# A decode block on Trainium2: the first 1,024 columns of w_o loaded in 12 DMAs of 5 to 18 rows instead of as part of one DMA of 128 rows

## The chip, the cores and the metric

The kernel runs on one core of one Trainium2 chip. The metric is device time in microseconds (us) of one execution, 376.72 us before the change, the median of two runs (376.61 and 376.82). Inside the core, work is issued by separate engines: TensorE (PE in the profile, its weight loads PEld), VectorE (DVE), ScalarE (ACT), GpSimd (POOL), and SyncE (SP), whose queue here does nothing but start DMAs. The data is moved by 16 DMA engines; the profile gives their mean busy share.

## The reference

Two tokens (B = 2) of width D = 448 go through one decode step. All data is fp32.

```python
xn = layernorm(x)                                   # no scale, no shift
q  = (xn @ wq)        -> 16 heads of 256             # wq: 448 x 4096
scores = q . k_cache^T / 16; p = softmax(scores)    # 8 kv heads, 4096 positions, 2 query heads share one kv head
o  = p . v_cache                                    # k_cache, v_cache: 2 x 8 x 4096 x 256 each
s  = o @ wo                                         # wo: 4096 x 448
g  = silu(((xn @ w_gate) * (xn @ w_up)) @ w_down)   # 448 x 1792, 448 x 1792, 1792 x 448
out = x + s * g
```

Almost all of the data is the two caches: 2 x 8 x 4096 x 256 x 4 B = 67 MB each, read once, 134 of the 158.5 MB that the kernel reads.

## The kernel before

There are 16 units of attention, one for each kv head and token, numbered i = 0 to 15. For a unit the keys are a [128, 8192] tile and the values another. The host packs the values of unit i beside the keys of unit i + 1, so that one DMA of [128, 16384] fp32 (8.4 MB, a row of 65,536 bytes for each of 128 partitions) brings both; there are 14 of these, named `vk` in the profile. They go into the pool `ring`, which has two buffers. The first keys (`first`), and the last keys and values (`last0`, `last1`, in 2 and 7 pieces), come apart. The weights (`wq0`, `w_gate` with `w_up`, `w_down`, `wq1` with a small piece `wqx`, `wo`) go one after the other through the pool `slot`, which has one buffer.

All these loads are started on one queue, SP's, by `issue()` (L73 and L77 of the profile), which takes them from a list `todo` in the order in which `plan()` (below it) has put them there. `wo` stands in the list behind the load of v8 and k9 and ahead of the load of v9 and k10. It is a [128, 10752] tile: 24 blocks of 448 columns, one block for each 128 rows of the reference's wo.

The schedule is written by hand (`manual_schedule`): each engine runs its instructions in the order of the code. Semaphores and waits are not in the code; the tile framework adds them, for data that must have arrived, for buffers that must be free, and for its own semaphores. A DMA that must wait holds up what stands behind it on SP.

In pass i of the main loop PE multiplies the probabilities of unit i with its values (`values`, L274), then the queries with the keys of unit i + 1 (`scores`, L243), then `issue()` puts the next load or two on SP's queue; the load into a ring buffer waits for the scores that free it. DVE and ACT compute the softmax of unit i + 1 beside this. In pass 7 the loads `wo` and v9 with k10 are put on the queue, in pass 8 the load of v10 with k11. `wo` is first used at the end of pass 8, by `project` (L301), 16 blocks, and again behind the loop. After the loop come the last two units, the last projections and the output store (L373), which SP starts.

Of the kernel before, what the change touches and what calls it, by code (L numbers as in the profile page):

```python
# [13 lines left out]
B, D = 2, 448  # L14
# [12 lines left out]
LATE = 24  # L27
# [2 lines left out]
SIDE = 16  # L30
EXTRA = 8
EPS = 1e-5

# [4 lines left out]
def gated_decode_block(ctx: ExitStack, tc: tile.TileContext, x, first, vk, last0, last1, wq0, wq1, wqx, wo, wgu, wd, out):  # L40
    nc = tc.nc
# [20 lines left out]
    def issue(n=1):  # L62
        for names, src, cuts in todo[:n]:
            weight = names[0].startswith("w")
            if weight:
                t = slot.tile([128, PART], F32, name="slot", align_bytes=512)
            else:
                t = ring.tile([128, 2 * ROW], F32, name="ring", align_bytes=512)
            width = ROW if not weight else PART // len(names)
            for i, name in enumerate(names):  # L70
                loaded[name] = t[:, i * width:(i + 1) * width]
            for lo, hi in zip(cuts, cuts[1:]):
                nc.sync.dma_start(t[:, lo:hi], src[:, lo:hi])  # L73
            if names == ["wq1"]:
                at = src.shape[1]
                loaded["wqx"] = t[:, at:at + EXTRA * 512]
                nc.sync.dma_start(loaded["wqx"][:SIDE], wqx[:, :4])  # L77
        del todo[:n]

    def plan(names, src, cuts=None):  # L80
        todo.append((names.split(), src, cuts or [0, src.shape[1]]))

    plan("wq0", wq0)
    plan("k0", first)
    weights = {0: ("wg wu", wgu), 2: ("wd", wd), 4: ("wq1", wq1), 8: ("wo", wo)}
    for i in range(LAST):
        plan(f"v{i} k{i + 1}", vk[i])
        if i in weights:
# [1 line left out]
    plan(f"k{LAST + 1} v{LAST}", last0, [0, ROW, 2 * ROW])  # L90
    plan(f"v{LAST + 1} wo2", last1, [0, 4096, 7168, *(ROW + i * D for i in (0, 3, 5, 7, 8))])
    issue(3)


# [20 lines left out]
    nc.vector.scalar_tensor_tensor(sq, xc, 1.0, xc, op0=OP.mult, op1=OP.mult, accum_out=st[:, 2:3])  # L115
    nc.vector.tensor_scalar(st[:, 3:4], st[:, 2:3], 1.0 / D, EPS, op0=OP.mult, op1=OP.add)
    rstd = const.tile([B, 1], F32)
# [16 lines left out]
    for j in range(NK):  # L134
        at = 384 + j * SIDE
# [65 lines left out]
    def lift(ps):  # L201
        t = work.tile([128, D], F32, name="h")
        nc.scalar.copy(t, ps[:, :D])
        return t
# [108 lines left out]
    oT2 = const.tile([128, 1, 2, REP, W], F32)  # L313
    ss = scores(0)
    issue(2)
    p = over(softmax(*ss))
    for i in range(LAST):
        g, b = divmod(i, B)
        o = bank("o", 1)
        values(i, p[0], o)  # L320
        ss = scores(i + 1)

        issue(1 + (i + 1 in weights))
        nc.scalar.activation(ob[:, b * 4 + g if g < 4 else b * 3 + g - 4], o, AF.Copy, scale=p[1])  # L324
        if i == LAST - 1:
            cb = combine(ob, 6)
        p = softmax(*ss)
        if i < LAST - 1:
            p = over(p)
        if i == 7:  # L330
            cb = combine(ob, 8)
            for n in range(B):
                turn(oT0, cb[:, n * 256:(n + 1) * 256], 0, n, 4)
            ob = work.tile([128, 8, 512], F32, name="ob", bufs=1)
        if i in weights:
            if i == 0:
                ffn_in()
            if i == 2:
                ffn_out()
            if i == 4:  # L340
                query(1)
            if i == 8:
                project(oT0, 0, 0, EARLY)
# [6 lines left out]
    t = lift(wide)  # L350
# [72 lines left out]
```

## Time and profile before

The profiled execution took 376.59 us, of which 374.8 us is the span from its first instruction to its last.

| | |
|---|---|
| time, median of 2 runs | 376.72 us (376.61 to 376.82) |
| profiled execution | 376.59 us |
| its span | 374.8 us |
| read from memory | 158.54 MB, mean 424 GB/s over the span |
| PE busy | 207.3 us, 55% of the span |
| PEld, DVE, ACT busy | 61.8, 63.2, 36.2 us |
| POOL busy | 1.2 us |
| the chain that ended last | DMA 79%, PE 19%, SP's queue 1% |

The page has a strip of 40 slices with the busy share of each engine and of the DMA engines, a list of groups of instructions with the time that the engine waited ahead of them and for whom, and the chain of work that ended last. Other views list the instructions of one engine by time, who waited for whom, and, for chosen stretches of time, the busy time of each engine, the mean share of the 16 DMA engines and the rate. A DMA packet is counted in the stretch in which it starts, so that a short stretch can show a share over 1.

### The profile page before, as it was taken

How to read it: one execution, taken by the hardware profiler on the slowest of the kernel's cores; microseconds unless marked ns; L12 is line 12 of the kernel's file. 1: busy time of each engine (PE TensorE's matmuls, PEld its weight loads, DVE VectorE, ACT ScalarE, POOL GpSimd, SP SyncE). 2: the span in 40 equal slices, each digit the busy share in tenths (PEclk: the TensorE clock that was granted, in tenths of full speed). 3: DMA queues.
4: the chain of work that ended last, by engine and by line, in shares of the span. 5: the costliest groups of instructions: out<-in, count | busy, mean ns of one | idle time of the engine just before them, and what ended most of it. 6: DMA issues, size and time to landing. Idle time of an engine off the chain costs nothing.

```text
span 374.8 us, 3254 instructions
## 1 busy us (share of the span) xinstructions
PE 207.3 (55%) x1464; PEld 61.8 (16%) x1464; DVE 63.2 (17%) x113; ACT 36.2 (10%) x56; POOL 1.2 (0%) x7
## 2 busy tenths in 40 slices
PE   1550648081762928678374666642718191909775
PEld 0110112020210202112121211200202020202222
DVE  4012030103030030300303030300211203020530
ACT  1001020001012020100101010200010101010120
POOL 1000000000000000000000000000000000000000
PEclk9987596778686667886758695865968776877999
DMA  8999999998999999999999999999999999999994
GB/s 340 440 465 399 430 453 448 448 442 377 428 442 441 441 403 465 414 448 435 427 448 441 442 415 407 440 448 448 441 428 421 441 441 413 435 416 437 411 418 168
DMA packets 4245, 158.74 MB, mean 424 GB/s; under 512 B 502, under 2 KB 632, under 8 KB 1144
## 3 DMA queue, kind: packets, MB, share of 16 engines
q1 hardware_dynamic: 4228, 158.54, 98.1%
q8 instruction: 11, 0.18, 0.2%
q14 instruction: 2, 0.02, 0.0%
q10 hardware_dynamic: 4, 0.00, 0.0%
HBM read 158.54 MB, written 0.01 MB: 423 GB/s over the span
## 4 chain that ended last, share of the span: by engine, by line
DMA 79%; PE 19%; SPq 1%; issue 0%; DVE 0%
DMA ring<-vk 68%; PE o L274 11%; PE s L243 8%; DMA ring<-first 5%; DMA ring<-last 5%; SPq L73 1%; PE acc L307 0%; DVE h L371 0%; DVE h L372 0%
## 5 line engine op out<-in xcount | busy, mean ns | idle before, releaser
L274 PE MATMUL o<-ring,pT 128*32 128x512 f32 x480 | 84.5, 868 | 88.0 <-DMA ring<-vk 88.0
L243 PE MATMUL s<-ring,qT 128*32 128x512 f32 x512 | 59.7, 607 | 6.0 <-DMA ring<-first 4.5
L244 DVE TENSOR_REDUCE m<-s 128x1 f32<-128x1024 f32 x16 | 19.6, 1225 | 221.2 <-PE s L243 221.2
L274 PEld LDWEIGHTS o<-ring,pT 128*32 128x32 f32 x480 | 21.2, 152 | 142.9 <-issue 142.9
L324 ACT ACTIVATE ob<-o,su 128x512 f32<-128x512 f32 x14 | 9.6, 688 | 194.3 <-PE o L274 194.3
L258 ACT ACTIVATE p<-s,m 128x1024 f32<-128x1024 f32 x16 | 17.8, 1113 | 95.2 <-DVE m L255 95.2
L243 PEld LDWEIGHTS s<-ring,qT 128*32 128x32 f32 x512 | 17.5, 112 | 45.4 <-issue 43.7
L260 DVE STREAM_TRANSPOSE pT<-p 128x1024 f32<-128x1024 f32 x16 | 19.9, 1246 | 22.5 <-ACT p L258 22.5
L266 PE MATMUL sm<-su,add_head 128*128 128x1 f32 x32 | 7.1, 292 | 22.9 <-ACT p L258 22.9
L249 PE MATMUL sm<-ident,m 128*1 128x128 f32 x16 | 4.3, 270 | 18.9 <-DVE m L244 18.8
L251 DVE TENSOR_REDUCE mx<-sm 1x128 f32<-1x512 f32 x16 | 10.9, 679 | 6.3 <-PE sm L249 6.3
L171 PE MATMUL t<-slot,xnT 128*32 128x512 f32 x48 | 8.7, 877 | 4.2 <-DMA slot<-wq 4.2
L254 PE MATMUL sm<-one,mx 1*128 1x1 f32 x16 | 3.6, 226 | 12.4 <-DVE mx L251 12.4
L266 PEld LDWEIGHTS sm<-su,add_head 128*128 128x128 f32 x32 | 5.8, 226 | 25.1 <-ACT p L258 24.1
L171 PE MATMUL s<-slot,xnT 128*32 128x448 f32 x48 | 7.2, 748 | 2.5 <-DMA slot<-wgu 2.5
L301 PE MATMUL wide<-slot,oT 128*32 128x448 f32 x48 | 7.1, 740 | 0.0
L249 PEld LDWEIGHTS sm<-ident,m 128*1 128x1 f32 x16 | 1.3, 79 | 33.0 <-DVE m L244 32.3
L283 PE MATMUL cb<-ob,add_blocks 128*32 128x64 f32 (+2 forms) x64 | 5.4, 461 | 0.8 <-ACT ob L363 0.8
L177 PE MATMUL t<-slot,oT 16*32 16x512 f32 x16 | 5.5, 678 | 0.0
L193 DVE STREAM_TRANSPOSE qT<-t 128x256 f32<-128x256 f32 x4 | 1.6, 428 | 20.3 <-PE t L177 10.8
L274 PE MATMUL wide<-ring,pT 128*32 128x512 f32 x32 | 4.2, 600 | 1.2 <-DMA ring<-last 1.2
L225 PE MATMUL t<-slot,hT 128*32 128x448 f32 x28 | 4.9, 787 | 0.0
(70 smaller groups left out, 50.8 us busy)
## 6 DMA issues: line engine op xcount, KB each, us to landing
ring<-last SPq DMA_DIRECT2D x2, 4096.0 KB, 24.7
slot<-wgu SPq DMA_DIRECT2D x1, 6272.0 KB, 39.9
slot<-wo SPq DMA_DIRECT2D x1, 5376.0 KB
ring<-first SPq DMA_DIRECT2D x1, 4096.0 KB, 20.3
slot<-wq SPq DMA_DIRECT2D x1, 3584.0 KB, 11.1
slot<-wq SPq DMA_DIRECT2D x1, 3328.0 KB, 35.1
slot<-wd SPq DMA_DIRECT2D x1, 3136.0 KB, 36.6
ring<-last SPq DMA_DIRECT2D x1, 2048.0 KB
```

The costliest lines, as they stand in the source:

```text
L171: nc.tensor.matmul(ps[W * c:W * (c + 1), :n], xnT[:, k, :], block(NT * k + c), start=k == 0, stop=False)
L177: nc.tensor.matmul(ps[W * c:W * (c + 1), :n], xeT[:, j, :], extra[:SIDE, at:at + n], start=False, stop=j == NK - 1)
L243: nc.tensor.matmul(s[W * c:W * (c + 1), h, :], q[:, d], k[:, h, d, c, :], start=d == 0, stop=d == 1)
L244: nc.vector.tensor_reduce(m[:, 0:1], s, axis=AX.XY, op=OP.max)
L249: nc.tensor.transpose(sm[:1, :128], m[:, 0:1], ident)
L251: nc.vector.tensor_reduce(mx, sm[:1, None, :128].rearrange("p o (c j) -> p o j c", c=NT).to_broadcast([1, NT, W, NT]), axis=AX.X, op=OP.max)
L258: nc.scalar.activation(p, s, AF.Exp, bias=m[:, 1:2], scale=1.0 / 16, accum_out=su[:, 0:1])
L260: nc.vector.transpose(pT.rearrange("p h n -> p (h n)"), p.rearrange("p h n -> p (h n)"))
L266: nc.tensor.matmul(sm[:, 130:131], add_head.rearrange("p a r j -> p (a r j)"), su[:, 0:1], start=True, stop=True)
L274: nc.tensor.matmul(o[W * t:W * (t + 1), :], pT[:, h, at:at + 2 * W:2], loaded[f"v{i}"][:, e * 512:(e + 1) * 512], start=e < NT, stop=e >= ...
L301: nc.tensor.matmul(wide[W * t:W * (t + 1), :D], heads(oT, i, first), loaded["wo"][:, i * D:(i + 1) * D], start=i < NT, stop=i >= LATE - NT)
L324: nc.scalar.activation(ob[:, b * 4 + g if g < 4 else b * 3 + g - 4], o, AF.Copy, scale=p[1])
```

## The change

The columns 0 to 1023 of the `wo` tile are cut off from the rest. They are loaded by 12 DMAs that each take some of the 128 rows: 5, 6, 7, and so on up to 15, and then 18 rows (their sum is 128), 4,096 bytes for each row. The other 9,728 columns follow as one DMA of 128 rows (38,912 bytes each). The bytes are the same, and so are the place in the list and every computation.

```diff
+NARROW = 1024
+ROWS = [*range(5, 16), 18]
...
             for lo, hi in zip(cuts, cuts[1:]):
-                nc.sync.dma_start(t[:, lo:hi], src[:, lo:hi])
+                if names == ["wo"] and lo == 0:
+                    at = 0
+                    for some in ROWS:
+                        nc.sync.dma_start(t[at:at + some, lo:hi], src[at:at + some, lo:hi])
+                        at += some
+                else:
+                    nc.sync.dma_start(t[:, lo:hi], src[:, lo:hi])
...
-    weights = {0: ("wg wu", wgu), 2: ("wd", wd), 4: ("wq1", wq1), 8: ("wo", wo)}
+    weights = {0: ("wg wu", wgu), 2: ("wd", wd), 4: ("wq1", wq1), 8: ("wo", wo, [0, NARROW, LATE * D])}
```

## The prediction

> **What bounds the kernel now.** I first ask which engine's work fills the span. The page's chain of work that ended last, and the groups with the largest waits, say that it is the loads:
>
> ```profile
> DMA 79%; PE 19%; SPq 1%; issue 0%; DVE 0%
> DMA ring<-vk 68%; PE o L274 11%; PE s L243 8%; DMA ring<-first 5%; DMA ring<-last 5%; SPq L73 1%; PE acc L307 0%; DVE h L371 0%; DVE h L372 0%
> ...
> L274 PE MATMUL o<-ring,pT 128*32 128x512 f32 x480 | 84.5, 868 | 88.0 <-DMA ring<-vk 88.0
> ```
>
> PE stood still for 88 us ahead of `values` until a load had landed. The 19% of PE in the chain do not say that PE is a limit in part: they are the stretches in which the chain runs from a landed load through PE to the buffer that becomes free. Whether the DMA engines ever stood still is in the view of busy time by stretches:
>
> ```profile
> 0.00:1.70 1.70, 0.00 (x0) 0.00 (x0) 0.09 (x2) 0.39 (x1) 0.70 (x6) 1.00 0.00 1
> 1.70:366.00 364.30, 202.97 (x1372) 59.75 (x1376) 62.35 (x108) 35.16 (x55) 0.55 (x1) 0.76 1.00 432
> ```
>
> From 1.7 us to 366 us the share is 1.00 at 432 GB/s: there is always a next load behind the one that is running. So the end is set by bytes, by any hole in the DMA stream, and by how unevenly the 16 engines finish. The last is seen at the end, stretch by stretch (the columns ahead of the last two belong to other engines; the share is the last but one):
>
> ```profile
> 366.00:367.50 1.50, 1.50 (x16) 0.38 (x8) 0.00 (x0) 0.00 (x0) 0.00 (x0) 1.00 1.03 407
> 367.50:369.00 1.50, 0.71 (x23) 0.35 (x25) 0.00 (x0) 0.69 (x1) 0.00 (x0) 1.00 0.75 299
> 369.00:370.00 1.00, 1.00 (x48) 0.79 (x36) 0.25 (x1) 0.00 (x0) 0.00 (x0) 1.00 0.47 190
> 370.00:371.00 1.00, 0.61 (x24) 0.35 (x16) 0.00 (x0) 0.00 (x0) 0.00 (x0) 1.00 0.21 79
> ```
>
> The first engines run dry soon after 367.5 us, the last shortly before 371. The mean engine still has 1.5 x 0.75 + 0.47 + 0.21 = 1.8 us of work after 367.5, to 369.3, so the last is some 1.5 us behind the mean and 3.3 us behind the first. More than 1.5 us is not to be had from evening out the engines.
>
> **The change: the SP queue.** The bytes stay. What is added is 12 DMAs on SP's queue, ahead of the load of v9 and k10. Their place in time, and PE's side of it:
>
> ```profile
> 199.86 0.33 SPq L73 DMA_DIRECT2D ring<-vk  x1
> 200.28 0.39 SPq L73 DMA_DIRECT2D slot<-wo  x1
> 218.05 0.33 SPq L73 DMA_DIRECT2D ring<-vk  x1
> ```
> ```profile
> ring<-vk SPq DMA_DIRECT2D x1, 28.4
> ```
> ```profile
> 228.39 6.05 PE L274 MATMUL o<-ring,pT 128*32 128x512 f32 x32 [2.83 <-DMA ring<-vk]
> 234.26 3.62 PE L243 MATMUL s<-ring,qT 128*32 128x512 f32 x32
> ...
> 242.59 5.35 PE L301 MATMUL wide<-slot,oT 128*32 128x448 f32 x32
> 260.38 4.99 PE L274 MATMUL o<-ring,pT 128*32 128x512 f32 x28 [12.43 <-DMA ring<-vk]
> ```
>
> The load of v8 and k9 starts at 199.86 and lands 28.4 us later, at 228.3. `wo` is on the queue from 200.28 and fills the engines behind it; v9 with k10 is added at 218.05. If issuing were all, 12 more at under 1 us each would be through by 212, ahead of 218, and cost nothing. The question is whether SP may issue 13 DMAs in a row at all. The end of the kernel answers it:
>
> ```profile
> SPq L373 <- DMA ring<-last: 5.5, 1, 5.5
> ```
> ```profile
> 327.36 24.16 SPq L73 DMA_DIRECT2D ring<-last  x9
> 372.21 0.58 SPq L373 DMA_DIRECT2D res<-h  x1
> ```
> ```profile
> L373 SPq EVENT_SEMAPHORE  x1: 17/17/17, 357.1 to 357.1; - x1
> ```
>
> L373 is the output store. It reads the result that DVE writes, no byte of `ring`; still it waited 5.5 us, until 357.1, for a load into `ring`. Of the nine last loads, two were issued at 327.4 and seven from 347.3 on; a load still under way at 357.1 with no use for the store is one of the first two, and the store is the eighth DMA behind the second of them. I read this as: the DMAs share eight semaphores in turn, and a DMA may not be issued before the one that had its semaphore, eight places earlier, has landed. Before the change that hurts nowhere, because a DMA is eight places behind only when long landed.
>
> In the changed kernel it binds. Counting the parts as 1 to 12 and the rest as 13: the DMA eight places ahead of part 8 is the load of v8 and k9 itself (part 7 has v7 with k8, landed at about 209). So SP stands at part 8 until 228.3. Behind it wait parts 9 to 12, the rest, and v9 with k10, which misses its slot of 218.05. Parts 9 to 13 wait for parts 1 to 5, which were issued early and land within a microsecond or so of 228.3. Meanwhile the engines have only parts 1 to 7, 56 rows of 4 KB or 0.23 MB, 0.5 us at 432 GB/s, instead of 12.7 us of `wo`: they run dry.
>
> **The price of the hole.** From 228.3 SP issues parts 8 to 12, then the rest. The rows for one issue:
>
> ```profile
> 114.49 0.33 SPq L73 DMA_DIRECT2D slot<-wq  x1
> 114.86 0.82 SPq L77 DMA_DIRECT2D slot<-wqx  x1
> ```
> ```profile
> 347.65 0.43 SPq L73
> 348.08 0.05 issue
> 348.13 0.43 SPq L73
> 348.56 0.04 issue
> 348.60 1.49 SPq L73
> 350.09 0.04 issue
> 350.13 0.43 SPq L73
> ```
> ```profile
> 0.74 0.53 ACTq L100 DMA_DIRECT2D pT<-x  x1
> ```
>
> A full-height load costs 0.33 to 0.43 us and a gap of 0.05; one in the row took 1.49. The two of few rows, as the parts are, took 0.82 (16 rows) and 0.53 (2 rows, on ScalarE's queue). I take 0.55 with the gap on top: 5 x 0.60 = 3.0 us, so the rest is issued at 231.3 (bounds: 0.33 and 0.82 each, 230.2 and 232.7). Then it starts on idle engines. The price of that is in the first load of the kernel:
>
> ```profile
> slot<-wq SPq DMA_DIRECT2D x1, 3584.0 KB, 11.1
> ...
> res<-h SPq DMA_DIRECT2D x1, 7.0 KB, 1.7
> ```
>
> 3,584 KB at 432 GB/s are 8.5 us, and it landed after 11.1: 2.6 us over. The store, all latency, landed after 1.7. I take 2.4, near the load, which is of the same kind (bounds 1.7 and 2.6). [...]
>
> The rest is 128 x 38,912 bytes, 4.98 MB, 11.5 us at 432 GB/s. It lands at 231.3 + 2.4 + 11.5 = 245.2. Before, `wo` came straight behind v8 and k9, so its last engine finished 5,376 KB or 12.7 us after 228.3, at 241.0. That is 4.2 us later for the last engine.
>
> Evenness enters here once. At 228.3 the 16 engines were apart as at the end, by some 3 us; the restart puts them level, so the engines that led lose more than 4.2 and the last one that. After it they drift apart again, for one by the instruction loads:
>
> ```profile
> q8 instruction: 11, 0.18, 0.2%
> ```
>
> Eleven of 16 KB; 0.2% of 16 engines' span is 12 us, about 1.1 us each. One that hits an engine which lagged by nothing now counts, where it was hidden behind the laggards before. I add 1.1 (bounds 0 and 1.4, the latter if an engine lags at the restart too): **5.3 us** in all, bounds 2.4 (230.2 + 1.7 + 11.5 - 241.0) and 7.2 (232.7 + 2.6 + 11.5 - 241.0 + 1.4).
>
> Nothing later gives it back: the share of 1.00 leaves no slack in the stream. v9 with k10 goes on the queue right behind the rest, in time. PE is not in the way: `project` at 242.59 will wait until about 246, needs 5.35 us, and PE had 12.43 us to spare before v9 landed. The load of v10 and k11 waits for `scores` at 234.26, which depends on v8 and k9 and is not moved. The order at the end is the same.
>
> Small terms: the parts move 0.52 MB in 4 KB packets. In 366.0 to 367.5, where packets are small too, the rate was 407 against 432 at full share, so 6% of 1.2 us, under 0.1. PE has more semaphores to wait for ahead of `project`, in its slack.
>
> Sum: 376.59 + 5.3 = 381.9; the profiled execution is 0.13 below the median of the two runs, so **382.0**, or 1.4% slower. A difference under 2% (7.5 us) is about what a measurement of this kernel tells from no change.
>
> **The rivals.** (a) SP is not held, because the eight in turn is a misreading or the waits fall otherwise: the 5.5 us at L373 speak against it. Then only the balance counts. Parts of 5 to 15 and 18 rows can't be even over 16 engines: one that takes a row of each part, and two of the 18, has 13 of 4 KB instead of 128/16 = 8. It loses 5 x 4,096 bytes at 432/16 = 27 GB/s, 0.76 us, and if the late engines are such ones the time is 377.4. [...] No row here names engines. (b) Faster: SP is not held and the late engines are those that get none of the 8 packets they had. They gain 8 x 4,096 bytes, 1.2 us: 375.5. It decides where the last engine at 370.8 is one that the parts leave out; the limit is the 1.5 us between last and mean. (c) Much slower: the framework takes the parts, which write the same columns of one tile in different rows, for overlapping writes and lets each wait for the one before it to land. From 228.3 that is 12 round trips of at least 1.7 us, 20 us, then the rest: 228.3 + 20.4 + 2.4 + 11.5 = 262.6 against 241.0, so 398. `wqx` writes rows of a tile beside another DMA without a wait, but in other columns.
>
> **How the numbers follow.** Forecast 382.0: 0.75. (a) 0.12, (b) 0.05, (c) 0.08. The forecast's own bounds are 379.0 and 383.8, with one issue of 1.49 us among the six 384.8. The range 377.2 to 384.3 holds (a) and nearly all of the forecast. Slower by over 2% is over 384.3: (c) and 0.07 of the forecast, 0.15. Faster by over 2% has no mechanism here: 0.01.
>
> **What would show it.** In the changed trace: SP's queue issues seven parts from 200 to 210, then waits for `ring<-vk` until 228.3, then five parts and the rest by 231 to 233; the DMA share falls well under 1 between 226 and 234; v9 with k10 is issued after 231, and lands near 265 rather than 260. If the issue of v9 with k10 stays at 218, (a) or (b) holds; if the parts come one every 2 us from 228, (c). The forecast is wrong in size if the issues of few rows are much dearer than 0.55 us, or if the engines restart faster than 2.4 us.

## The result, and the profile after

The changed kernel takes 382.76 us (two runs, 382.71 and 382.82) against 376.72: 1.0161 times the time before, 95% interval 1.0145 to 1.0178, or 6.0 us more. The span of its profiled execution is 380.8 us instead of 374.8.

SP's queue in order of time (start, length, line, operation; L79 issues the parts, L82 the other loads), and the waits of that queue between 196 and 275 us:

```profile
198.73 0.33 SPq L82 DMA_DIRECT2D ring<-vk  x1
199.15 31.70 SPq L79 DMA_DIRECT2D slot<-wo  x12
230.90 0.35 SPq L82 DMA_DIRECT2D slot<-wo  x1
231.35 43.16 SPq L82 DMA_DIRECT2D ring<-vk  x3
```
```profile
SPq L79 <- DMA ring<-vk: 27.5, 2, 19.6
```

The 12 parts take 31.7 us to issue, of which 27.5 are two waits for loads into `ring`, the longer 19.6 us. The rest of `wo` is issued at 230.90, and v9 with k10 at 231.35, where it was 218.05 before. The chain that ended last, first before, then after, shows the queue as part of the path here, where before it went straight from PE to the load:

```profile
218.03 0.02 issue
218.05 42.19 DMA ring<-vk
260.24 0.14 issue
```
```profile
198.73 30.21 DMA ring<-vk
228.94 0.02 issue
228.96 0.30 SPq L79
229.25 0.04 issue
229.30 0.36 SPq L79
...
230.90 0.35 SPq L82
...
231.35 34.16 DMA ring<-vk
265.51 0.14 issue
```

The load of v8 and k9 landed at 228.94, part 8 followed at 228.96, and the load of v9 and k10 landed at 265.51 instead of 260.24. What the DMA engines did meanwhile, by stretches (the last two columns are their mean share and the rate in GB/s), first before, then after:

```profile
224.00:226.00 2.00, 1.56 (x8) 0.00 (x0) 0.39 (x2) 0.00 (x0) 0.00 (x0) 0.50 0.68 293
226.00:228.00 2.00, 0.00 (x0) 0.00 (x0) 0.39 (x2) 0.00 (x0) 0.00 (x0) 0.50 1.29 559
228.00:230.00 2.00, 1.61 (x8) 0.45 (x12) 0.00 (x0) 0.00 (x0) 0.00 (x0) 0.50 0.89 387
230.00:232.00 2.00, 2.00 (x16) 0.67 (x12) 0.00 (x0) 0.00 (x0) 0.00 (x0) 0.50 0.84 366
```
```profile
224.00:226.00 2.00, 2.00 (x16) 0.39 (x8) 0.04 (x1) 0.00 (x0) 0.00 (x0) 0.50 0.58 225
226.00:228.00 2.00, 0.91 (x8) 0.00 (x0) 0.78 (x2) 0.00 (x0) 0.00 (x0) 0.61 0.11 43
228.00:230.00 2.00, 0.92 (x12) 0.41 (x16) 0.00 (x0) 0.00 (x0) 0.00 (x0) 1.00 0.21 64
230.00:232.00 2.00, 2.00 (x24) 0.73 (x20) 0.00 (x0) 0.00 (x0) 0.00 (x0) 1.00 0.68 185
```

A packet counts where it starts, so two-microsecond stretches jump about their mean; but a share of 0.11 and then 0.21, at 43 and 64 GB/s, is a hole. The end of the changed kernel, to be compared with the rows of 366 to 371 in the prediction:

```profile
372.50:374.00 1.50, 1.06 (x8) 0.15 (x4) 0.00 (x0) 0.39 (x1) 0.00 (x0) 1.00 1.02 402
374.00:375.00 1.00, 0.65 (x35) 0.65 (x39) 0.15 (x1) 0.30 (x1) 0.00 (x0) 1.00 0.69 271
375.00:376.00 1.00, 0.86 (x32) 0.49 (x23) 0.10 (x1) 0.00 (x0) 0.00 (x0) 1.00 0.27 104
376.00:377.00 1.00, 0.67 (x20) 0.46 (x24) 0.00 (x0) 0.00 (x0) 0.00 (x0) 1.00 0.03 13
```

The mean engine has 0.69 + 0.27 + 0.03 = 1.0 us of work after 374, so it ends at 375.0, 5.7 us later than before; the last is some 1.5 us behind it, as before. The loss is a delay of all the engines.

### The profile page after: what moved, and what is told of

Read it like the earlier page. It is cut to its first block, busy times and chain, and to the rows that moved or that the text cites. A ratio compares the mean times of both kernels' runs of the same rounds, so it can differ in the third digit from the quotient of the medians.

```text
span 380.8 us, 3270 instructions
## 1 busy us (share of the span) xinstructions
PE 213.2 (56%) x1464; PEld 63.5 (17%) x1464; DVE 63.2 (17%) x113; ACT 36.2 (10%) x56; POOL 1.2 (0%) x7
## 3 DMA queue, kind: packets, MB, share of 16 engines
q1 hardware_dynamic: 4475, 158.54, 96.9%
## 4 chain that ended last, share of the span: by engine, by line
DMA 80%; PE 17%; SPq 2%; issue 0%; DVE 0%
DMA ring<-vk 74%; PE o L283 11%; PE s L252 6%; DMA ring<-last 5%; SPq L82 1%; SPq L79 0%; PE acc L316 0%; DVE h L380 0%; DVE h L381 0%
## 5 line engine op out<-in xcount | busy, mean ns | idle before, releaser
L283 PE MATMUL o<-ring,pT 128*32 128x512 f32 x480 | 83.2, 856 | 86.0 <-DMA ring<-vk 85.1
L252 PE MATMUL s<-ring,qT 128*32 128x512 f32 x512 | 61.4, 622 | 5.5 <-DMA ring<-first 4.0
L253 DVE TENSOR_REDUCE m<-s 128x1 f32<-128x1024 f32 x16 | 19.6, 1225 | 224.9 <-PE s L252 224.9
L310 PE MATMUL wide<-slot,oT 128*32 128x448 f32 x48 | 8.7, 774 | 4.5 <-DMA slot<-wo 4.4
L186 PE MATMUL t<-slot,oT 16*32 16x512 f32 x16 | 7.4, 942 | 0.0
L263 PEld LDWEIGHTS sm<-one,mx 1*128 1x128 f32 x16 | 2.2, 138 | 15.4 <-DVE mx L260 15.4
```

Source lines behind the costliest of these rows:

```text
L186: nc.tensor.matmul(ps[W * c:W * (c + 1), :n], xeT[:, j, :], extra[:SIDE, at:at + n], start=False, stop=j == NK - 1)
L252: nc.tensor.matmul(s[W * c:W * (c + 1), h, :], q[:, d], k[:, h, d, c, :], start=d == 0, stop=d == 1)
L253: nc.vector.tensor_reduce(m[:, 0:1], s, axis=AX.XY, op=OP.max)
L283: nc.tensor.matmul(o[W * t:W * (t + 1), :], pT[:, h, at:at + 2 * W:2], loaded[f"v{i}"][:, e * 512:(e + 1) * 512], start=e < NT, stop=e >= ...
L310: nc.tensor.matmul(wide[W * t:W * (t + 1), :D], heads(oT, i, first), loaded["wo"][:, i * D:(i + 1) * D], start=i < NT, stop=i >= LATE - NT)
```

## The experiments

All of them are changes to the load of `wo`, or add a small load beside it; the computation is untouched. The kernel before was run again beside each group, at 376.65 to 376.78 us; ratios and losses are against that. The first question was whether the hole goes when SP is no longer held, and whether the parts cost anything by themselves.

**Six parts, and seven.** The rest of `wo` is the seventh DMA behind v8 and k9 in one kernel, the eighth in the other.

```diff
-ROWS = [*range(5, 16), 18]
+ROWS = [5, 10, 15, 20, 39, 39]           # six
+ROWS = [5, 6, 10, 14, 15, 39, 39]        # seven
```

> Six uneven parts (5, 10, 15, 20, 39, 39 rows) of the first 1,024 columns, then the rest as the seventh DMA. Theory (SP is held at the DMA eight places behind the load of v8 and k9): the rest is the seventh, so it is issued at about 209 and covers the engines; the load of v9 and k10 is held instead until about 229, which costs nothing. No hole in the DMA share between 224 and 236, 376.3 to 377.8 us. Rival, parts of few rows are slow in themselves: half of the change's loss, 379.5 to 380.

> Seven uneven parts (5, 6, 10, 14, 15, 39, 39 rows), then the rest as the eighth DMA. Theory: the rest is now the held one, issued at about 229.0 instead of 230.9 in the changed kernel, so 1.9 us less than it: 380.5 to 381.2, a step of 3 to 4 us from six parts to seven. Rival, parts of few rows are slow in themselves: 380, a step of 0.5 us from six to seven.

Measured: six parts 380.87 us (1.0108 times the time before, 1.0093 to 1.0123), seven 381.90 (1.0135, 1.0120 to 1.0150). SP's queue, first with six, then with seven:

```profile
199.77 2.16 SPq L79 DMA_DIRECT2D slot<-wo  x6
209.12 0.35 SPq L82 DMA_DIRECT2D slot<-wo  x1
231.36 63.24 SPq L82 DMA_DIRECT2D ring<-vk  x4
```
```profile
200.18 9.25 SPq L79 DMA_DIRECT2D slot<-wo  x7
230.11 0.36 SPq L82 DMA_DIRECT2D slot<-wo  x1
```

The hold is where the theory put it: as the seventh DMA the rest of `wo` is issued at 209, as the eighth at 230. The time misses its range by 0.7 us with seven parts, and by 3 with six: no hold in the way of `wo`, and still 4.1 us lost. The step from six to seven is 1.0 us, where 3 to 4 were expected. Something other than the hole costs about 4 us.

**All 12 parts, the rest seventh.** The same DMAs as in the change, in another order.

```diff
-                    for some in ROWS:
+                    for place, some in enumerate(ROWS):
+                        if place == 6:
+                            nc.sync.dma_start(t[:, hi:LATE * D], src[:, hi:])
                         nc.sync.dma_start(t[at:at + some, lo:hi], src[at:at + some, lo:hi])
                         at += some
-                else:
+                elif names != ["wo"]:
                     nc.sync.dma_start(t[:, lo:hi], src[:, lo:hi])
```

> All 12 parts of the change, with the same rows; only the rest is issued seventh, behind part 6, instead of thirteenth. Theory: the engines have the rest to work on while SP is held, so there is no hole: 376.5 to 378.2 (the upper end if the engines that take 13 rows are the late ones, 0.8 us). Rival, the parts are slow in themselves: 382.8 as in the changed kernel.

Measured: 381.46 us (1.0127, 1.0112 to 1.0142). Taking the hold off the path gives back 1.3 of the 6.0 us. The stretches show why:

```profile
226.00:228.00 2.00, 0.05 (x4) 0.00 (x0) 0.78 (x2) 0.00 (x0) 0.00 (x0) 0.50 0.85 291
228.00:230.00 2.00, 0.00 (x0) 0.00 (x0) 0.00 (x0) 0.00 (x0) 0.00 (x0) 0.50 0.96 311
230.00:232.00 2.00, 1.94 (x12) 0.68 (x16) 0.00 (x0) 0.00 (x0) 0.00 (x0) 0.50 0.82 337
```

There is no hole: the share is 0.82 to 0.96. But the engines, busy, move 291 to 337 GB/s instead of 432. The packets take longer (their lengths are in a table below). Both the theory (376.5 to 378.2) and its rival (as much as in the changed kernel, 382.8) miss; the measured time lies much nearer to the rival.

**Twenty parts.** `ROWS = [6] * 12 + [7] * 8`.

> Twenty parts (12 of 6 rows, 8 of 7) instead of 12. Theory: the rest is issued 13 issues of 0.36 us behind 228.95 instead of 5, at about 233.8 instead of 230.9: 2.9 us more than the changed kernel, 385.4 to 386.2, with the DMA share low for that much longer. A longer hole per part (over 0.5 us each, above 387) would say that each part also waits for the landing of an earlier one.

Measured: 385.44 us (1.0234, 1.0216 to 1.0251), 2.7 us more than the changed kernel. The rest is issued at 233.13 instead of 230.90:

```profile
233.13 0.35 SPq L82 DMA_DIRECT2D slot<-wo  x1
```

Here, where the engines are dry anyway, a further part costs about one issue, 0.3 us: as expected.

**The hold alone.** Twelve parts of full height, 128 columns each, ahead of the rest.

```diff
-    weights = {0: ("wg wu", wgu), 2: ("wd", wd), 4: ("wq1", wq1), 8: ("wo", wo)}
+    weights = {0: ("wg wu", wgu), 2: ("wd", wd), 4: ("wq1", wq1), 8: ("wo", wo, [*range(0, 1537, 128), LATE * D])}
```

> Twelve full-height parts (128 rows of 128 columns, the first 1,536 columns) and then the rest: the hold of the SP queue with no part of few rows. Theory: the hole alone. Released at 228.3, five issues of 0.42 us, the rest (4.7 MB, 10.9 us) 3 us behind its issue: landed at about 244.5 instead of 241, and 1 us for evenness: 380.3 to 381.7, with a DMA share well under 1 between 226 and 232. Rival, the hold is harmless and the rows were the cost: 376.5 to 377.2.

Measured: 382.01 us (1.0140, 1.0123 to 1.0157), 5.4 us, just over the range. SP, and the stretches:

```profile
199.63 31.51 SPq L73 DMA_DIRECT2D slot<-wo  x13
```
```profile
226.00:228.00 2.00, 1.36 (x8) 0.00 (x0) 0.58 (x2) 0.00 (x0) 0.00 (x0) 0.50 0.43 125
228.00:230.00 2.00, 1.45 (x8) 0.46 (x12) 0.20 (x1) 0.00 (x0) 0.00 (x0) 0.50 0.27 80
```

So a hold with no part of few rows costs nearly as much as the whole change. Not all of the 5.4 us is the hole, though: these parts come in 1,536 packets of 512 bytes and 28 ns, 2.7 us for each engine, where the same bytes would take 1.8 us at 432 GB/s. The account further below has 3.1 us of it as standing still.

**Which rows, and how many engines.** Eight parts of 16 rows that lie together, eight parts of 16 rows that lie eight apart (both with the rest seventh), and two halves of 64 rows with the rest behind them.

```diff
-ROWS = [*range(5, 16), 18]
+ROWS = [16] * 8                          # sixteen, together; the rest seventh, as above
...
+nc.sync.dma_start(t[place:128:8, lo:hi], src[place:128:8, lo:hi])   # sixteen, apart
...
+ROWS = [64, 64]                          # halves
```

> Eight parts of 16 rows that lie together, the rest issued seventh, so no hole. Each of the 16 engines should have one row of each part: the shares are even, 8 packets for each engine as before. Theory now (several engines that write rows lying close together get in each other's way): still slow, 379.5 to 381, with a DMA share near 1 and a low rate from 224 on. [...] Rival, uneven shares of the engines were what cost: now even, 376.5 to 377.2.

> As the run with eight parts of 16 rows, but each part takes every eighth row (n, n + 8, n + 16, ...), so the same bytes, packets, shares and order, with the rows of a part spread over the height. Theory: by spreading them fewer engines meet, so clearly faster than the run with rows lying together, by 1 to 3 us: 377.5 to 379. Rival, what costs is the number of DMAs or of small packets, or the reading side: the same time as with rows lying together, within 0.5 us.

> Two parts of 64 rows and the rest, three DMAs: no hold, no hole, even shares. Theory (engines meet where a DMA covers a part of the height): 64 rows lying together are half of the height, so half the rate for 0.52 MB, 1.2 us more: 377.5 to 378.5. Rival, only DMAs of few rows cost: 376.6 to 377.1.

Measured: together 380.83 us (1.0107, 1.0091 to 1.0122), apart 380.28 (1.0095, 1.0080 to 1.0110), halves 380.90 (1.0110, 1.0095 to 1.0125). Shares that should be even, an estimate from 16 rows and 16 engines (the trace names no engines), do not save it, so on that estimate uneven shares were not the main cost. Spreading the rows was to gain 1 to 3 us and gained 0.55, with overlapping intervals: that expectation failed. And two DMAs of half the height, with SP never held, cost 4.25 us where I had 1.2 and the rival less than 0.5. SP with halves, and the stretches:

```profile
200.48 1.16 SPq L79 DMA_DIRECT2D slot<-wo  x2
201.69 0.58 SPq L82 DMA_DIRECT2D slot<-wo  x1
```
```profile
224.00:226.00 2.00, 1.73 (x10) 0.00 (x0) 0.23 (x1) 0.00 (x0) 0.00 (x0) 0.50 0.85 236
226.00:228.00 2.00, 0.00 (x0) 0.00 (x0) 0.55 (x2) 0.00 (x0) 0.00 (x0) 0.50 0.77 197
228.00:230.00 2.00, 0.00 (x0) 0.00 (x0) 0.00 (x0) 0.00 (x0) 0.00 (x0) 0.50 1.33 301
230.00:232.00 2.00, 0.96 (x8) 0.37 (x12) 0.00 (x0) 0.00 (x0) 0.00 (x0) 0.50 0.76 216
```

**A quarter of the bytes in halves**, with `NARROW = 256`.

> As the run with two halves of 64 rows, but of the first 256 columns instead of 1,024: a quarter of the bytes, the same three DMAs. Theory (engines that write the same stretch of rows at the same time slow each other, in proportion to the bytes): a quarter of the loss of 4.25 us, 377.4 to 378.2. Rival, a DMA that isn't of full height costs a fixed time, however small: 380 to 381.

Measured: 377.43 us (1.0024, 1.0010 to 1.0038), 0.72 us instead of 4.25. A fixed price of 3 to 4 us for a DMA that is not of full height is ruled out; between these two runs the loss goes about with the bytes.

**The same extra load into rows 0 to 15, and into rows 64 to 79.** The kernel before, with one more small DMA into columns that nothing reads. Only the rows written differ; the diff shows the line of each of the two kernels. With rows 0 to 15 its 16 packets stand in the trace as four chains of four, one packet right behind the other, which I read as four engines carrying it.

```diff
+            if names == ["wo"]:
+                nc.sync.dma_start(t[0:0 + SIDE, LATE * D:], wqx[:, :4, :PART - LATE * D])    # rows 0 to 15
+                nc.sync.dma_start(t[64:64 + SIDE, LATE * D:], wqx[:, :4, :PART - LATE * D])  # rows 64 to 79
```

> The kernel before, with one more load behind wo: 16 rows of 7,168 bytes into rows 0 to 15 of columns that nothing reads, from the source of wqx, cut in fours as wqx is. It adds work, 0.11 MB on four engines, 1.06 us each. [...] Theory: only these four get later, 376.7 to 378.0, and the packets of the full-height loads keep their lengths (1,589 and 2,418 ns). Rival, any DMA of few rows disturbs the others: 378 to 379.5 with longer packets beside it, as much as with rows 64 to 79.

> As the run with the extra load, into rows 64 to 79 instead of 0 to 15: the same DMA, bytes, engines and source. Theory: the same four engines now write where four others write in the full-height load, so both are slowed while it runs, and the packets beside it are longer: 1 to 2 us more than with rows 0 to 15, 378 to 379.5. Rival, what rows are written doesn't matter: the same time as with rows 0 to 15, within 0.4 us.

Measured: rows 0 to 15 377.96 us (1.0035, 1.0022 to 1.0048), rows 64 to 79 379.16 (1.0070, 1.0055 to 1.0085). The first is 1.25 us more than the kernel before, near the 1.06 us that I had estimated, its 0.11 MB on four engines; the second is another 1.2 us for the same bytes. PE's next wait for v9 and k10, first with rows 0 to 15, then with rows 64 to 79, and the stretch in which the extra load runs, in the same order:

```profile
261.56 5.17 PE L276 MATMUL o<-ring,pT 128*32 128x512 f32 x32 [13.11 <-DMA ring<-vk]
```
```profile
263.05 5.97 PE L276 MATMUL o<-ring,pT 128*32 128x512 f32 x32 [14.78 <-DMA ring<-vk]
```
```profile
241.00:243.00 2.00, 0.58 (x6) 0.57 (x10) 0.67 (x2) 1.21 (x2) 0.00 (x0) 0.50 1.08 470
```
```profile
241.00:243.00 2.00, 0.64 (x6) 0.62 (x10) 0.67 (x2) 1.20 (x2) 0.00 (x0) 0.50 0.95 342
```

The lengths of the single DMA packets in the two traces, and in some of the others, say it most plainly. They are the trace's packet records between 196 and 262 us, in ns; the last two columns count the 65,536-byte packets of the `vk` loads that took over 100 ns more than the shortest, 2,418, and the sum by which all of them exceeded it:

```
kernel                 wo, full height        the small parts        vk packets longer, sum us
                       bytes   min   mean     bytes  min  mean
before                 43,008  1,589 1,589    -                       2    1.1
changed                38,912  1,439 1,523    4,096  156  208        14    4.2
12 parts, rest seventh 38,912  1,439 1,637    4,096  159  207        41   31.9
extra, rows 0 to 15    43,008  1,589 1,589    7,168  272  272         2    1.1
extra, rows 64 to 79   43,008  1,589 1,589    7,168  272  384        22   15.5
halves, 1,024 columns  38,912  1,439 1,678    4,096  159  256        14   12.7
halves, 256 columns    41,984  1,552 1,603    1,024   46   48        12    4.2
twelve flat            36,864  1,361 1,470      512   25   28         3    1.7
```

With rows 0 to 15 no packet of the other loads, and none of its own, is lengthened (the two long ones are there before the change as well). With rows 64 to 79 there are twenty-two long ones, and its own are longer by 40% on average. The source, the bytes and the loads beside it are the same; rows 64 to 79 are not slow in themselves, since the full-height loads write them too, in packets of the shortest length (before, none of the 128 of `wo` took over 1,651 ns). So I read it as a matter of which rows are written beside which other packets; why the rows matter is not shown, and that the four engines met four others in rows 64 to 79 was only assumed, since the trace names no engines. (The longer `wo` packets of the flat parts and of the changed kernel are the first ones behind the hole.)

**The hold, covered.** `wo` in 12 DMAs of full height and 896 columns.

```diff
-    weights = {0: ("wg wu", wgu), 2: ("wd", wd), 4: ("wq1", wq1), 8: ("wo", wo)}
+    weights = {0: ("wg wu", wgu), 2: ("wd", wd), 4: ("wq1", wq1), 8: ("wo", wo, [*range(0, LATE * D + 1, 896)])}
```

> wo in 12 DMAs of full height, 896 columns each: SP is held at the eighth just as in the changed kernel, but the engines have 3.2 MB to move until then, and no DMA is of part of the height. Theory: the hold costs nothing where it is covered, 376.4 to 377.3. Rival, 12 more DMAs or the late load of v9 and k10 cost by themselves: 379 to 382.

Measured: 377.76 us (1.0026, 1.0015 to 1.0036). SP, and two stretches:

```profile
199.01 34.12 SPq L73 DMA_DIRECT2D slot<-wo  x12
233.97 56.21 SPq L73 DMA_DIRECT2D ring<-vk  x4
```
```profile
228.00:230.00 2.00, 1.39 (x8) 0.46 (x12) 0.00 (x0) 0.00 (x0) 0.00 (x0) 0.50 1.02 416
230.00:232.00 2.00, 2.00 (x13) 0.45 (x8) 0.00 (x0) 0.00 (x0) 0.00 (x0) 0.50 1.02 416
```

SP is held longer than in the changed kernel, v9 with k10 goes out at 233.97, and 1.05 us is lost, not 6.0: here a hold that was covered by bytes was nearly free. It missed its range (to 377.3) by 0.5 us. At a share of 1.02 the rate is 416 rather than 432 GB/s: `wo` now comes in 96 packets of 3,584 bytes and 140 ns for each engine, 13.4 us, instead of 8 of 1,589 ns, 12.7 us. That is 0.7 of the 1.05 us; the rest was not traced.

**Standing still, or busy for longer.** The packet records split each loss in two: how much longer the engines were busy (the lengths of all packets of the load queue, divided by 16) and how much longer they stood still between 196 and 262 us, both against the kernel before, beside the growth of the profiled span, in us (packets overlap a little in the records, so a small minus stands for none):

```
kernel                      span   busy   still
changed                     +6.0   +1.4   +4.2
twenty parts                +8.9   +1.4   +6.6
seven parts                 +5.5   +2.0   +3.1
twelve flat                 +5.3   +2.0   +3.1
six parts                   +4.5   +3.9   -0.1
12 parts, rest seventh      +5.4   +4.3   -0.1
16 rows, together           +4.1   +4.1   -0.1
16 rows, eight apart        +3.6   +3.6   -0.1
halves, 1,024 columns       +4.3   +3.6   -0.1
wo in 12 of 896 columns     +1.0   +0.8   -0.3
```

The line of the load queue on the page says the same more coarsely: 98.1% of 374.8 us busy before, 96.9% of 380.8 us in the changed kernel, 97.9% of 380.2 us with the rest seventh (before, changed, rest seventh):

```profile
q1 hardware_dynamic: 4228, 158.54, 98.1%
```
```profile
q1 hardware_dynamic: 4475, 158.54, 96.9%
```
```profile
q1 hardware_dynamic: 4475, 158.54, 97.9%
```

There are two separate losses: where the rest of `wo` is held and nothing covers the hold, the engines stand still (3.1 to 6.6 us longer); elsewhere they do not, and in the five kernels with parts of few or of half the rows longer packets make up most of the loss (3.6 to 4.3 of 3.6 to 5.4 us).

No kernel of these is faster than the one before.

## Why the prediction was right, and where it was not

The forecast was 382.0 in a range of 377.2 to 384.3; 382.76 lies in it, and the mechanism named, the hold and the hole behind it, is there: the engines stood still for 4.2 us longer. The nearness of the number proves less than it seems, for two reasons. With the hole taken away by the order of the DMAs the time is 381.46, inside the forecast's bounds as well; it is the issue times and the empty engines that show the hole. And v9 with k10 came 5.3 us late, just as in the sum, because errors in it nearly cancel: the release came 0.7 us later, the five issues took 1.1 us less, and the restart 0.2 us more. That part is luck.

- **SP is held at the eighth DMA.** Right: seven parts by 209, then the wait until v8 and k9 had landed, and the seventh and eighth place of the rest tell it apart (209 and 230). The reading of one wait, 5.5 us of the output store for a load that it did not need, carried this.
- **Released at 228.3.** Measured 228.96. The load of v8 and k9 itself took 30.2 us instead of 28.4, though it was issued 1.1 us earlier. In the changed kernel too `vk` packets of that time are longer: 14 of them, 4.2 us in sum. Parts 1 to 7 running beside them is the likely cause, by the runs with extra rows. The sum had no term for it.
- **Five issues at 0.60, 3.0 us.** Measured 228.96 to 230.90, 1.9 us: a part costs 0.30 to 0.38 us and a gap, and is no dearer than a full-height load (the rest: 0.35). The row to go by would have been the 0.33.
- **The restart at 2.4 and 1.1 for evenness, 3.5 us.** The rest and v9 with k10 are 13.37 MB, 30.9 us at 432 GB/s; issued at 230.90 they would land at 261.8 and did at 265.51: 3.7 us. The first packets of the rest start at 232.0, 1.1 us behind its issue, and take up to 2.5 us instead of 1.44. How the 3.7 us fall to restart and evenness was not separated. At the end the last engine was some 1.5 us behind the mean, as before. The account for two other holes came out at 385.4 for twenty parts, in its range, and at 382.0 for twelve flat parts, 0.3 us above it.
- **Small terms, under 0.1.** Too small: the 4,096-byte packets of the parts took 208 ns on average and 159 where nothing lengthened them, 0.4 us for each engine.
- **Nothing later gives it back.** Right; the 5.3 us by which v9 and k10 are late become 6.0 at the end.
- **Rivals (a) and (b): without the hold 377.4 or 375.5.** Wrong, and the weakest part of the text. The five kernels in which the engines always had work, with the same 0.52 MB in parts that are not of full height, cost 3.6 to 4.7 us. The step that failed is "then only the balance counts": the packets get longer, 3.6 to 4.3 us for each engine. I had not weighed what a part's rows may do to the packets beside it (the extra load cost 1.25 us in rows 0 to 15, 2.45 in rows 64 to 79). No run shows the shares that the two sums use, 13 packets on one engine in (a), none on another in (b), since no trace names engines; what the runs showed in their place is the longer packets. Between parts of 16 rows and the uneven ones (380.83 against 381.46, both with the rest seventh) there may be the 0.6 us of the balance; the intervals overlap.
- **Rival (c), each part waiting for the one before.** Wrong: five parts in 1.9 us.
- **Slips.** On 376.72 us rival (a) comes to 377.5, and the forecast's bounds to 379.1 and 383.9; each is given 0.1 lower. That under 2% can hardly be told from no change was too cautious: all runs of the kernel before lay between 376.49 and 377.16 us, and the interval of the change does not reach 1.

The two losses do not add: 5.4 for the hold with flat parts, 4.7 for the parts with the rest seventh, 6.0 for both. In the changed kernel 72 of the 128 rows run in the hole, beside few other packets, so the hole hides most of what they would cost: the engines are busy for 1.4 us longer instead of 4.3. Taking the hole away lets the parts meet the rest of `wo` and v9 with k10. That they meet is read from the packet lengths, not shown by a run of its own.

Open: why halves cost 4.25 us. Longer packets make up 3.6 of it, but why they are so long is not settled. The 1.2 us expected was an estimate, 0.52 MB at half of the rate, and no run shows the half. Also open is why rows eight apart gained next to nothing on rows lying together (0.55 us). The number of DMAs is not the cause (halves have two), nor the number of small packets (the quarter in halves has as many, 128, and lost 0.72 us). That reading has no part in it is shown only for the two extra loads, which read the same source and differ by 1.2 us.

## What to carry to other kernels

Count the DMAs between a load and the ones that must be issued before it lands: in this kernel the eighth waited for it on the issuing queue (the rest of `wo` was issued at 209 as the seventh, at 230 as the eighth), with everything behind it, and that was nearly free only where the bytes already queued covered the wait (1.05 us lost, against 5.4 with the flat parts). The runs show the count of eight, and the trace's records of the DMAs on SP's queue show eight semaphores in turn (102, 105 to 110, 100): part 8 has 110, as the load of v8 and k9. Keep big loads at full height and cut them by columns rather than rows: in the packet table the DMAs that cover part of the rows have 12 to 41 longer `vk` packets beside them, against 2 before, except the one with rows 0 to 15, with 2. When an experiment removes the cause that was named and the time stays, look at rate beside share: busy engines at 300 GB/s (a share of 0.82 to 0.96 at 291 to 337, with the rest seventh) are another fault than idle ones (0.11 and 0.21 at 43 and 64, in the changed kernel).

## What was not expected of the hardware

Two half-height DMAs of 0.26 MB each, in a stream of 158 MB, cost 4.25 us, not far from the 5.4 us of the hold with flat parts. A 16-row DMA of 0.11 MB cost 1.25 or 2.45 us, depending on nothing but its destination rows.
